# state @ w_in of batches 6 and 7: from a zero-padded stationary beside chunk 1 to eight float32 array tiles behind chunk 3

## The chip, the core and the metric

The kernel runs on one core of a Trainium2 chip. The metric is the device time of one execution in microseconds, the median of a few runs. Three runs of the kernel before took 663.02, 664.64 and 666.04 us. The core's engines work side by side, each through its own list of instructions in order: TensorE (PE, with its weight loads PEld), VectorE (DVE), ScalarE (ACT), GpSimd (POOL) and SyncE (SP), which issues nearly all DMAs.

## The reference

Attention between 512 tokens `x` and 32 state rows in both directions, for 8 batches and 8 heads, and then a feed-forward block over all rows.

```python
scores = x @ state^T / 8;  a  = softmax(scores);   xread = a  @ state   # B=8, H=8, S=512, D=64
scores2 = state @ x^T / 8; a2 = softmax(scores2);  sread = a2 @ x       # Ns=32
rows = concat([xread, sread])      # 544 rows a batch, 512 wide (8 heads x 64)
h = rows @ w_in                    # 512 -> 2048
out = (h - tanh(h)) @ w_out        # 2048 -> 512
```

## The kernel before

**What is multiplied.** For a token row, `xread @ w_in` is `a @ (state @ w_in)`. So the kernel makes `m = state @ w_in` for each batch (32 state rows by 8 heads, 2048 wide), and the first layer of a batch is `a @ m`: 256 rows are contracted where 512 would be. All products that need full precision are made from two float32r halves (`hi`, `lo`; `split`, line 99: a copy on ACT and a subtraction on DVE) as three matmuls.

**Chunks.** Batch i is chunk i. `Chunk.hidden(f)` (line 471) makes hidden block f of 16 with six matmuls of 128x512 (lines 483 to 485) into one of two `ps_h` banks, ACT takes tanh, DVE subtracts. `Chunk.output(f)` (lines 504 to 532) adds block f to four output banks with twelve matmuls. Chunks 0 to 3 run one after the other, step `st = 16 i + f`, two blocks ahead (`LAG`). Chunks 4 to 7 run in two `Pair`s (line 868) which share seven products instead of eight (`product`, line 944); their order is the list `ticks`. Chunk 8 holds the state rows of all batches.

**Where m comes from.** Blocks (q, k) of w_in, q = 0 to 3 and k = 0 or 1, are 128x1024 in the DRAM tiles `wf`. Batches 0 and 1 are done early: `m_first_two` (line 159) multiplies with plain float32 matmuls of 64 rows by 32 columns, four places in each of two banks of `ps_a`, eight instructions in all, followed by ACT copies. Batches 2 to 7 are done by `m_units` (line 205), 16 units, one for each (q, k, c): ACT and DVE split a 128x512 block of w_in (`wst`), six matmuls of 64x128 columns (line 232, `mps`) give batches 2 to 5, and three matmuls with the full array (line 239, `mls`) give batches 6 and 7. For these the stationary `sls` holds two heads on 128 rows with zeros where head and row do not belong together. ACT copies the banks out (`st`, line 197 through `free`; `sl`, line 241), and SP stores four pieces of `st` and four of `sl` to the DRAM tiles `md` (lines 247, 251). `load_m` (line 254) reads them back as `mr`, 512 KB for each (batch, q), and splits them to `m`. There is one `mr` buffer.

**What sets the order.** The program names a step for each side job: `ASIDE` (line 760) for chunks 0 to 3, `SIDES` (line 776) by tick for the pairs. A scheduler then orders the instructions of each engine by its own estimate, within priorities and explicit `issue_after` gates. `free` keeps all its ACT copies in one chain, and `behind_free` lets the first matmul of a group into `ps_a` wait for the last copy of that chain, since both banks must be free. The pools have few buffers: `stage` 2, `wf` 2, `x` 2 (tokens `xT` and `xn` of an attention, 512 KB each), `parts` 4 (the weights `W` of the pairs). SP issues DMAs in list order; one that waits holds all behind it. The attention of a batch is a generator: loads of `xT`, scores (`sps`, line 324, eight float32 matmuls of 64 rows by 32 columns), softmax, transposes (`pps`, line 410), loads of `xn`, the state read (`rps`, line 431).

Of the kernel before, what the change touches and what calls it, by code (L numbers as in the profile page):

```python
# [9 lines left out]
F32 = mybir.dt.float32  # L10
F32R = mybir.dt.float32r
# [8 lines left out]
P = 128  # L20
B, H, S, NS, D = 8, 8, 512, 32, 64
# [3 lines left out]
NQ = 4  # L25
# [6 lines left out]
TURN = (0, 1, 3, 2)  # L32
# [3 lines left out]
def attention_ffn(ctx: ExitStack, tc: tile.TileContext, xT, xn, bd, bh, sp, sm, sl, win, wout, xout, tout, sout):  # L36
# [62 lines left out]
    def split(hi, lo, src, sub=None):  # L99

        return nc.scalar.copy(hi, src), (sub or nc.vector).tensor_sub(lo, src, hi)  # L101
# [52 lines left out]
    def second(q):  # L154
        if q < 2:
            return pool.tile([P, 2, 512], F32, tag="stage", name=f"mr1{q}", bufs=SB)
        return pool.tile([P, 2, 512], F32, tag="g", name=f"mr1{q}", bufs=GB)

    def m_first_two(q, p):

        k = p // 2
        if p == 0:

            m_first[q] = pool.tile([P, 2, 512], F32, tag="mr", name=f"mr0{q}", bufs=RRB)
            m_second[q] = second(q)
        if p % 2 == 0:
            return
        pss = [bank(ps_a, f"mps0{q}{p - 1 + c}") for c in range(2)]
        run = []
        for b in range(2):  # L170
            for c in (1, 0):
                for e in range(2):
                    r = slice(64 * e, 64 * e + 64)
                    at = 64 * b + 32 * (e ^ c)
                    rows = slice(at, at + 32)
                    with ExitStack() as behind:
                        if run:
                            behind.enter_context(tc.issue_after(run[-1]))
                            behind.enter_context(tc.high_priority())
                        made = nc.tensor.matmul(  # L180
                            pss[c][rows], sps[r, p - 1 + c, rows], wfs[q, k][r, c], start=True, stop=True
                        )
                    if not run:
                        behind_free(made)
                    run.append(made.ins)
        for c in range(2):
            free(m_first[q][64 * c : 64 * c + 64, k], pss[c][0:64])
            free(m_second[q][64 * c : 64 * c + 64, k], pss[c][64:128])
# [16 lines left out]
    def m_units():  # L205
        raw = pool.tile([P, H, P], F32, tag="stage", name="smr", bufs=SB)
        s0 = pool.tile([P, 2, H, P], F32R, tag="sm", name="sms", bufs=1)
        nc.sync.dma_start(raw, sm)
        split(s0[:, 0], s0[:, 1], raw)
        raw = pool.tile([P, 4, P], F32, tag="stage", name="slr", bufs=SB)  # L210
        s1 = parts("sls", [P, 2, 4, P], F32R)
        nc.sync.dma_start(raw, sl)
        split(s1[:, 0], s1[:, 1], raw)
        for q in range(NQ):
            for k in range(2):
                w = pool.tile([P, 2, 512], F32, tag="wf", name=f"w1{q}{k}", bufs=WB)
                nc.sync.dma_start(w, wf[q][:, 2 * k : 2 * k + 2])
                for c in range(2):
                    p = 2 * k + c
                    t = twins(f"wst{q}{p}", [P, 2, 512], F32R)  # L220
                    split(t[:, 0], t[:, 1], w[:, c])
                    pss = [bank(ps_a, f"mps{q}{2 * p + e}") for e in range(2)]
                    ps2 = bank(ps_h, f"mls{q}{p}")
                    run = []
                    for n, (x, y) in enumerate(((0, 1), (0, 0), (1, 0))):
                        for e in (1, 0):
                            rows = slice(64 * e, 64 * e + 64)
                            with ExitStack() as behind:
                                if run:
                                    behind.enter_context(tc.issue_after(run[-1]))  # L230
                                    behind.enter_context(tc.high_priority())
                                made = nc.tensor.matmul(  # L232
                                    pss[e], s0[rows, x, 2 * p + e], t[rows, y], start=(n == 0), stop=(n == 2)
                                )
                            if not run:
                                behind_free(made)
                            run.append(made.ins)
                    for n, (x, y) in enumerate(((0, 0), (0, 1), (1, 0))):
                        nc.tensor.matmul(ps2, s1[:, x, p], t[:, y], start=(n == 0), stop=(n == 2))  # L239
                    late = pool.tile([P, 512], F32, tag="c2", name=f"sl{q}{p}", bufs=CSB)  # L240
                    nc.scalar.copy(late, ps2)
                    stage = pool.tile([P, 2, 512], F32, tag="stage", name=f"st{q}{p}", bufs=SB)
                    for e in range(2):
                        free(stage[:, e], pss[e])
                    for j in range(4):
                        dst = mdram[2 + j][q][k, 2 * c : 2 * c + 2]
                        nc.sync.dma_start(dst.rearrange("h n f -> n h f"), stage[32 * j : 32 * j + 32])
                    for e in range(2):
                        for j in range(2):
                            rows = slice(64 * e + 32 * j, 64 * e + 32 * j + 32)  # L250
                            nc.sync.dma_start(mdram[6 + j][q][k, 2 * c + e], late[rows])
                    yield

    def load_m(b, q):
        if b < 2:
# [33 lines left out]
    def attention(b, aT):  # L289
# [22 lines left out]
        def all_scores():  # L312

            pss.update({hf: bank(ps_a, f"sps{b}{hf}") for hf in range(2)})
            run = []
            for j in (2, 0, 3, 1):
                at = TURN[j] if b < 2 else j
                for hf in (1, 0):
                    rs = slice(64 * hf, 64 * hf + 64)
                    with ExitStack() as behind:  # L320
                        if run:
                            behind.enter_context(tc.issue_after(run[-1]))
                            behind.enter_context(tc.high_priority())
                        made = nc.tensor.matmul(
                            pss[hf][32 * at : 32 * at + 32], bdr[rs, j], xrs[j // 2][rs, j % 2], start=True, stop=True
                        )
                    if not run:
                        behind_free(made)
                    run.append(made.ins)
# [51 lines left out]
    def state_read(b, ss):  # L381
# [40 lines left out]
        for hf in range(2):  # L422
            for k in range(4):
                for c in range(4):
                    cs = slice(32 * c, 32 * c + 32)
                    j = TURN[c] if b < 2 else c
                    with ExitStack() as behind:
                        if run:
                            behind.enter_context(tc.issue_after(run[-1]))
                            behind.enter_context(tc.high_priority())  # L430
                        made = nc.tensor.matmul(  # L431
                            ps[cs, 64 * hf : 64 * hf + 64],
                            pts[hf][:, k, cs],
                            xrs[hf][:, k, 64 * j : 64 * j + 64],
                            start=(k == 0),
                            stop=(k == 3),
                        )
                    run.append(made.ins)
        for hf in range(2):
            for j in range(4):  # L440
                h = 4 * hf + (TURN[j] if b < 2 else j)
                js = slice(32 * j, 32 * j + 32)
                free(
                    sr[b // 4][32 * (b % 4) : 32 * (b % 4) + 32, 64 * h : 64 * h + 64],
                    ps[js, 64 * hf : 64 * hf + 64],
                    scale=ris[hf][js],
                )
# [308 lines left out]
    if "att0" in SCH:  # L756
# [3 lines left out]
    ASIDE = {  # L760
        "att1": D0["att"]["1"],
        "att2": [16 + x for x in (3, 4, 5, 6, 6, 8, 8, 9, 9)],
        "m0": [17, 18, 19, 20, 22, 23, 24, 25, 26, 27, 28, 29, 30, 31, 33, 34],
        "att3": [29, 30, 30, 31, 32, 33, 34, 35, 36],
        "a0": [37, 38, 38, 39],
        "att5": [39, 40, 40, 41, 42, 43, 44, 45, 46],
# [9 lines left out]
    SIDES = [  # L776
        {
            "att6": [0, 9, 14, 20, 26],
            "att7": [58, 61, 64, 67, 70, 73, 77, 81, 85],
        },  # L780
        {},
# [30 lines left out]
    def main(*made):  # L812
        mains[-1].extend(x.ins for x in made)

    late_units = {"a0": a0, "r1": late1, "m0": m1}

    def side(name, n=1):
        if not n:
# [290 lines left out]
```

## Time and profile before

| | |
|---|---|
| median of three runs | 664.64 us |
| profiled execution | 662.42 us, span 660.6 us, granted clock 0.992 |
| ACT busy | 389.2 us (59%), 675 instructions |
| PE busy | 633.5 us (96%), 3482 instructions |
| DVE busy | 483.8 us (73%) |
| DMA | 137.01 MB, mean 207 GB/s |
| lines 239 / 241 (`mls`) | 48 matmuls, 14.5 us; 16 ACT copies, 9.5 us |
| stores `md<-sl` / `md<-st` | 64 of 64 KB / 64 of 128 KB |

A row of the profile names line, engine, operation, tile written and tiles read. Times are microseconds from the span's start. A matmul of 128x512 is shown as 0.39 us long, but in a dense stream the next starts 0.23 us later, since matmuls are pipelined: PE time is read from start to start. A float32 matmul appears as two records in the trace. A row such as "x16" merges records that follow each other.

### The profile page before, as it was taken

The page shows a single profiled execution, that of the slowest core. Times are in us where ns is not written, and L with a number is a line of the kernel's source. Part 1 is how long each engine was busy: PE and PEld are TensorE (multiplying, and loading weights), DVE is VectorE, ACT ScalarE, POOL GpSimd, SP SyncE. Part 2 cuts the span into 40 slices and gives each one's busy share as a digit, 9 for nine tenths or more (in the row PEclk, how much of TensorE's full clock was granted, in tenths as well). Part 3 has the DMA queues.
Part 4 walks back from the last instruction along what each step waited for, and adds up shares of the span by engine and source line. Part 5 has one row for each costly group of instructions (what it writes and reads, how often), then busy time and mean ns, then how long its engine had stood idle before and what let it go on. Part 6 is the DMA issues. An engine that isn't in the chain of part 4 may idle for free.

```text
span 660.6 us, 9657 instructions
## 1 busy us (share of the span) xinstructions
PE 633.5 (96%) x3482; PEld 494.4 (75%) x3482; DVE 483.8 (73%) x769; ACT 389.2 (59%) x675; POOL 27.3 (4%) x41
## 2 busy tenths in 40 slices
PE   5879989999999999999999999999999999999997
PEld 2546667677777778787878887778888888788996
DVE  5999999639457876799637886996965789754442
ACT  3768875657667666576645576355655553543532
POOL 2000000000000000000000000000000000343300
PEclk9799999999999999999999999999999999999999
DMA  9799798356787974656722436464566535899800
GB/s 314 213 357 321 268 368 275 138 185 177 223 265 223 301 221 160 193 168 220 257 97 96 143 128 209 159 197 128 160 189 190 159 128 174 291 320 356 270 23 32
DMA packets 65199, 137.01 MB, mean 207 GB/s; under 512 B 6784, under 2 KB 28544, under 8 KB 65152
## 3 DMA queue, kind: packets, MB, share of 16 engines
q1 hardware_dynamic: 62592, 128.02, 59.5%
q0 software_dynamic: 2560, 8.39, 3.7%
q8 instruction: 27, 0.44, 0.3%
q14 instruction: 20, 0.16, 0.1%
HBM read 93.91 MB, written 42.47 MB: 206 GB/s over the span
## 4 chain that ended last, share of the span: by engine, by line
PE 77%; DVE 14%; DMA 4%; issue 3%; ACT 2%; SPq 0%; ACTq 0%; DVEq 0%
PE X L944 12%; PE hps L483 9%; PE hps L484 8%; PE hps L485 8%; PE ops L532 8%; PE ops L531 8%; PE ops L530 8%; PE Y1m L944 5%; PE Y0m L944 4%; PE mps L232 2%; PE mls L239 2%; PE rps L431 1%; DVE m L101 1%; DMA wo3d<-in_wout 1%; DVE w L131 1%
## 5 line engine op out<-in xcount | busy, mean ns | idle before, releaser
L531 PE MATMUL ops<-wo,g 128*128 128x512 f32 x256 | 99.9, 394 | 6.0 <-DVE wo L101 6.0
L483 PE MATMUL hps<-aT,m 128*128 128x512 f32 x248 | 99.3, 402 | 3.3 <-DVE G L497 1.3
L484 PE MATMUL hps<-aT,m 128*128 128x512 f32 x248 | 97.0, 391 | 0.0
L485 PE MATMUL hps<-aT,m 128*128 128x512 f32 x248 | 96.3, 391 | 0.0
L530 PE MATMUL ops<-wo,g 128*128 128x512 f32 x256 | 94.1, 396 | 0.9 <-ACT wo L101 0.8
L532 PE MATMUL ops<-wo,g 128*128 128x512 f32 x256 | 90.5, 394 | 0.0
L499 DVE TENSOR_TENSOR t<-hps,t 128x512 f32<-128x512 f32 (+1 forms) x78 | 49.5, 634 | 51.6 <-ACT t L499 51.3
L497 ACT ACTIVATE t<-hps 128x512 f32<-128x512 f32 x64 | 38.3, 599 | 61.8 <-PE hps L485 59.5
L497 DVE TENSOR_TENSOR G<-hps,t 128x512 f32<-128x512 f32 x64 | 43.9, 688 | 36.9 <-ACT t L497 36.9
L499 ACT ACTIVATE t<-hps 128x512 f32<-128x512 f32 (+1 forms) x78 | 43.3, 555 | 44.9 <-PE hps L485 42.3
L101 ACT CAST g<-t 128x512 fp32r<-128x512 f32 (+1 forms) x78 | 44.8, 579 | 32.0 <-DVE t L499 31.8
L483 PEld LDWEIGHTS hps<-aT,m 128*128 128x128 f32 x248 | 46.4, 188 | 22.9 <-ACT m L101 3.6
L531 PEld LDWEIGHTS ops<-wo,g 128*128 128x128 f32 x256 | 48.2, 188 | 19.0 <-DVE wo L101 8.3
L101 DVE TENSOR_TENSOR g<-t,g 128x512 fp32r<-128x512 f32 (+1 forms) x78 | 49.2, 633 | 14.8 <-ACT g L101 14.4
L530 PEld LDWEIGHTS ops<-wo,g 128*128 128x128 f32 x256 | 47.7, 188 | 16.4 <-ACT wo L101 3.0
L532 PEld LDWEIGHTS ops<-wo,g 128*128 128x128 f32 x256 | 48.2, 189 | 11.1 <-issue 0.8
L485 PEld LDWEIGHTS hps<-aT,m 128*128 128x128 f32 x248 | 46.5, 188 | 10.3 <-DVE m L101 0.4
L484 PEld LDWEIGHTS hps<-aT,m 128*128 128x128 f32 x248 | 46.6, 188 | 8.9
L982 POOL DMA_DIRECT2D wl<-wod x32 | 23.4, 730 | 590.9 <-DVE g1m L101 556.4
L944 PE MATMUL X<-g0m,W0m 128*128 128x512 f32 x192 | 46.9, 390 | 0.5 <-DVE g0m L101 0.5
L944 PE MATMUL X<-g1m,W1m 128*128 128x512 f32 x192 | 45.9, 391 | 0.6 <-DVE g1m L101 0.6
L101 ACT CAST g1m<-G 128x1024 fp32r<-128x1024 f32 x28 | 29.2, 1054 | 28.9 <-PE Y1m L944 12.7
(257 smaller groups left out, 1128.2 us busy)
## 6 DMA issues: line engine op xcount, KB each, us to landing
mr<-md SPq DMA_DIRECT2D x24, 512.0 KB, 3.8
xT<-in_xT SPq DMA_DIRECT2D x16, 512.0 KB, 4.9
wod<-wo SPq DMA_DIRECT2D x32, 256.0 KB, 6.1
md<-st SPq DMA_DIRECT2D x64, 128.0 KB, 2.4
xn<-in_xn SPq DMA_DIRECT2D x16, 512.0 KB, 5.3
wsd<-ws SPq DMA_DIRECT2D x16, 512.0 KB, 4.8
W0m<-wsd SPq DMA_DIRECT2D x16, 512.0 KB, 4.0
W1m<-wsd SPq DMA_DIRECT2D x16, 512.0 KB, 4.5
```

What stands on the lines that cost most here:

```text
L101: return nc.scalar.copy(hi, src), (sub or nc.vector).tensor_sub(lo, src, hi)
L232: made = nc.tensor.matmul(pss[e], s0[rows, x, 2 * p + e], t[rows, y], start=(n == 0), stop=(n == 2))
L483: nc.tensor.matmul(ps, mhi[k][:, cols], ahi[:, k], start=(k == 0), stop=False)
L484: nc.tensor.matmul(ps, mhi[k][:, cols], alo[:, k], start=False, stop=False)
L485: made = nc.tensor.matmul(ps, mlo[k][:, cols], ahi[:, k], start=False, stop=(k == nk - 1))
L497: main(nc.scalar.activation(t, ps, AF.Tanh), nc.vector.tensor_sub(g, ps, t))
L499: tanhs.append((nc.scalar.activation(t, ps, AF.Tanh).ins, nc.vector.tensor_sub(t, ps, t).ins))
L530: nc.tensor.matmul(o, g[:, 0, tok], w[:, 0], start=(f == 0), stop=False)
L531: nc.tensor.matmul(o, g[:, 0, tok], w[:, 1], start=False, stop=False)
L532: return nc.tensor.matmul(o, g[:, 1, tok], w[:, 0], start=False, stop=(f == NFF - 1)).ins
L944: made = nc.tensor.matmul(out[t], w[:, e, x, cols], y[:, e], start=first and j == 0 and e == 0 and c == 0, stop=last and j == 3 and e == 1 ...
L982: nc.gpsimd.dma_start(wo[f][:, :, cols].bitcast(F32), wod[:, f % 2, half, f // 2])
```

## The change

The three `mls` matmuls, the copy `sl`, its four stores and the padded stationary leave `m_units`. Batches 6 and 7 get a generator of their own, `m_last_two`, with a load step and then eight units, one for each (q, k). A unit has eight plain float32 matmuls of 64 rows by 32 columns into both `ps_a` banks (the code of `m_first_two`, now a function `eight`), two ACT copies of 128x512 into a `stage` tile, four stores of 128 KB, and the load of the next block of w_in (512 KB, `wf` pool). The stationary `spl` (128x256, not padded) lies in a buffer of the `x` pool. The units are asked for in the first pair's ticks 0 to 32, so the scheduler may place them from the end of chunk 3 on. The order of heads `TURN` that batches 0 and 1 had now holds for all batches, and the list of steps for the 16 units of `m_units` is 21 instead of 30 in one place.

```diff
-    def m_first_two(q, p):
+    def eight(name, held, w):
+        pss = [bank(ps_a, f"mps{name}{c}") for c in range(2)]
         run = []
         for b in range(2):
             for c in (1, 0):
...
-                        made = nc.tensor.matmul(
-                            pss[c][rows], sps[r, p - 1 + c, rows], wfs[q, k][r, c], start=True, stop=True
-                        )
+                        made = nc.tensor.matmul(pss[c][rows], held(c, r, rows), w[r, c], start=True, stop=True)
...
-        raw = pool.tile([P, 4, P], F32, tag="stage", name="slr", bufs=SB)
-        s1 = parts("sls", [P, 2, 4, P], F32R)
-        nc.sync.dma_start(raw, sl)
-        split(s1[:, 0], s1[:, 1], raw)
...
-                    ps2 = bank(ps_h, f"mls{q}{p}")
...
-                    for n, (x, y) in enumerate(((0, 0), (0, 1), (1, 0))):
-                        nc.tensor.matmul(ps2, s1[:, x, p], t[:, y], start=(n == 0), stop=(n == 2))
-                    late = pool.tile([P, 512], F32, tag="c2", name=f"sl{q}{p}", bufs=CSB)
-                    nc.scalar.copy(late, ps2)
...
-                    for e in range(2):
-                        for j in range(2):
-                            rows = slice(64 * e + 32 * j, 64 * e + 32 * j + 32)
-                            nc.sync.dma_start(mdram[6 + j][q][k, 2 * c + e], late[rows])
+    def m_last_two():
+        def held_w(q, k):
+            w = pool.tile([P, 2, 512], F32, tag="wf", name=f"w2{q}{k}", bufs=WB)
+            nc.sync.dma_start(w, wf[q][:, 2 * k : 2 * k + 2])
+            return w
+        spl = pool.tile([P, 4, 2, NS], F32, tag="x", name="spl", bufs=XB)
+        nc.sync.dma_start(spl, sl)
+        units = [(q, k) for q in range(NQ) for k in range(2)]
+        following = held_w(*units[0])
+        yield
+        for n, (q, k) in enumerate(units):
+            w = following
+            pss = eight(f"l{q}{k}", lambda c, r, rows: spl[r, 2 * k + c, rows.start // 64], w)
+            stage = pool.tile([P, 2, 512], F32, tag="stage", name=f"sl{q}{k}", bufs=SB)
+            for c in range(2):
+                free(stage[:, c ^ 1], pss[c ^ 1])
+            for b in range(2):
+                for c in range(2):
+                    dst = mdram[6 + b][q][k, 2 * c : 2 * c + 2]
+                    nc.sync.dma_start(dst.rearrange("h n f -> (h n) f"), stage[64 * b : 64 * b + 64, c])
+            if n < 7:
+                following = held_w(*units[n + 1])
+            yield
...
-        "m0": [17, 18, 19, 20, 22, 23, 24, 25, 26, 27, 28, 29, 30, 31, 33, 34],
+        "m0": [17, 18, 19, 20, 21, 22, 23, 24, 25, 26, 27, 28, 29, 31, 33, 34],
...
             "att6": [0, 9, 14, 20, 26],
+            "m6": [0, 4, 8, 12, 16, 19, 23, 29, 32],
...
-    late_units = {"a0": a0, "r1": late1, "m0": m1}
+    late_units = {"a0": a0, "r1": late1, "m0": m1, "m6": m_last_two()}
```

The change also moves instructions whose code it does not touch. In the rows below the numbers in a name are the program's own (`hps2_12` is hidden block 12 of chunk 2; `mps36`, `mps37` are the two banks of the last unit of `m_units`, q = 3), the number after the underscore is a running one, and the changed kernel's lines are 15 or 16 higher in this part of the file.

**First place, PE in chunk 2.** Before, the last matmul of the last unit of `m_units` is followed by hidden blocks 6 to 11 and outputs 4 to 9, some 106 rows, until the first matmul that reads `m23`, which that unit has to deliver:

```order
L232 MATMUL mps36_2297<-wst33_2294,sms_1134 128x512
L483 MATMUL hps2_6_2390<-aT2_1254,m21_2278 128x512
...
L532 MATMUL ops2_3_2197<-wo9_812,g2_9_2570 128x512
L483 MATMUL hps2_12_2736<-aT2_1254,m23_2733 128x512
L484 MATMUL hps2_12_2736<-aT2_1254,m23_2733 128x512
```

In the changed program the same unit stands behind output 9, and only outputs 10 and 11 (24 matmuls) and the transposes and state read of batch 3 are left between:

```order
L230 MATMUL mps36_2142<-wst33_2139,sms_1134 128x512
L545 MATMUL ops2_0_2049<-wo10_823,g2_10_2478 128x512
...
L547 MATMUL ops2_3_2052<-wo11_859,g2_11_2542 128x512
L425 MATMUL pps31_2198<-ident_72,s31_1918 128x128 x4
L425 MATMUL pps30_2197<-ident_72,s30_1916 128x128 x4
L446 MATMUL rps3_2238<-xn30_2193,p2t31_2209 32x64 x16
L446 MATMUL rps3_2238<-xn31_2195,p2t30_2207 32x64 x16
L498 MATMUL hps2_12_2571<-aT2_1229,m23_2568 128x512
```

The unit moved some five outputs later against hidden block 12, which itself now stands behind output 11 and not behind output 9.

**Second place, PE in the first pair.** The state read of batch 6 has two halves, `xn60` and `xn61`. Before, they stand together:

```order
L944 MATMUL X01_3816<-g0m130_3973,W0m13_3809 128x512
L431 MATMUL rps6_4112<-xn60_4025,p2t61_4041 32x64 x16
L431 MATMUL rps6_4112<-xn61_4027,p2t60_4039 32x64 x16
L483 MATMUL hps5_3_4043<-aT5_2614,m50_3959 128x512
```

In the changed program they stand 18 matmuls apart (six of `hps5_8`, six of a product, six of `hps5_9`), because `spl` holds one of the two `x` buffers and `xn61` goes into that of `xn60`:

```order
L446 MATMUL rps6_4065<-xn60_3959,p2t61_3975 32x64 x16
L498 MATMUL hps5_8_4130<-aT5_2449,m52_4062 128x512
...
L500 MATMUL hps5_9_4166<-aT5_2449,m52_4062 128x512
L446 MATMUL rps6_4065<-xn61_3961,p2t60_3973 32x64 x16
L498 MATMUL hps5_10_4177<-aT5_2449,m52_4062 128x512
```

**Third place, SP in the first pair.** Before, SP's list holds loads of `mr` and of pair weights `W0m` there:

```order
L259 DMA mr51_4010<-md51_94 128x2x512
L893 DMA W0m21_3924<-wod_77 128x1024
L893 DMA W0m22_3988<-wod_77 128x1024
L259 DMA mr52_4107<-md52_95 128x2x512
```

In the changed program the loads of w_in (`w2qk`) and the stores of the new units (`slqk`) stand among them; a store stands behind a weight load that waits until PE has used up a buffer:

```order
L264 DMA md60_97<-sl01_3745 64x512 x2
L264 DMA md70_101<-sl01_3745 64x512 x2
L274 DMA mr51_3925<-md51_94 128x2x512
L909 DMA W0m21_3820<-wod_77 128x1024
L247 DMA w220_3890<-wf2_107 128x1024
L264 DMA md61_98<-sl10_3811 64x512 x2
L264 DMA md71_102<-sl10_3811 64x512 x2
L247 DMA w221_3947<-wf2_107 128x1024
L909 DMA W0m22_3903<-wod_77 128x1024
L264 DMA md61_98<-sl11_3883 64x512 x2
```

Eight loads of 512 KB and 32 stores of 128 KB were added in this part, and 64 stores of 64 KB went from chunks 1 and 2.

More of the change, by code (lines that the diff above doesn't have):

```diff
@@ L157, in second @@
         return pool.tile([P, 2, 512], F32, tag="g", name=f"mr1{q}", bufs=GB)
-    def m_first_two(q, p):
[L161 to L168, printed above, removed]
+    def eight(name, held, w):
+        pss = [bank(ps_a, f"mps{name}{c}") for c in range(2)]
         run = []
@@ L185, in m_first_two @@
                     run.append(made.ins)
+        return pss
+    def m_first_two(q, p):
+        k = p // 2
+        if p == 0:
+            m_first[q] = pool.tile([P, 2, 512], F32, tag="mr", name=f"mr0{q}", bufs=RRB)
+            m_second[q] = second(q)
+        if p % 2 == 0:
+            return
+        pss = eight(f"0{q}{k}", lambda c, r, rows: sps[r, p - 1 + c, rows], wfs[q, k])
         for c in range(2):
@@ L237, in m_units @@
                             run.append(made.ins)
-                    for n, (x, y) in enumerate(((0, 0), (0, 1), (1, 0))):
-                        nc.tensor.matmul(ps2, s1[:, x, p], t[:, y], start=(n == 0), stop=(n == 2))
-                    late = pool.tile([P, 512], F32, tag="c2", name=f"sl{q}{p}", bufs=CSB)
-                    nc.scalar.copy(late, ps2)
                     stage = pool.tile([P, 2, 512], F32, tag="stage", name=f"st{q}{p}", bufs=SB)
                     for e in range(2):
-                        free(stage[:, e], pss[e])
+                        free(stage[:, e ^ c], pss[e])
                     for j in range(4):
@@ L316, in all_scores @@
             for j in (2, 0, 3, 1):
-                at = TURN[j] if b < 2 else j
+                at = TURN[j]
                 for hf in (1, 0):
@@ L425, in state_read @@
                     cs = slice(32 * c, 32 * c + 32)
-                    j = TURN[c] if b < 2 else c
+                    j = TURN[c]
                     with ExitStack() as behind:
@@ L440, in state_read @@
             for j in range(4):
-                h = 4 * hf + (TURN[j] if b < 2 else j)
+                h = 4 * hf + (TURN[j])
                 js = slice(32 * j, 32 * j + 32)
@@ L1085 @@
     sm = c(np.broadcast_to(sT[2:6].transpose(2, 1, 0, 3).reshape(1, D, H, P), (2, D, H, P)).reshape(P, H, P))
-    sl = np.zeros((2, D, 4, 2, 2, NS), x.dtype)
-    for e in range(2):
-        sl[e, :, :, e] = sT[6:, e::2].transpose(2, 1, 0, 3)
-    sl = sl.reshape(P, 4, P)
+    sl = c(sT[6:].reshape(2, 4, 2, D, NS).transpose(2, 3, 1, 0, 4).reshape(P, 4, 2, NS))
     win, wout = (c(w).view(np.int64) if w.dtype == np.float64 else w for w in (moe_w_in, moe_w_out))
```

## Prediction

> **What bounds the kernel now.** I read the page's busy times and slices first, then the busy time by stretches, then PE's timeline from start to start.
>
> ```profile
> PE 633.5 (96%) x3482; PEld 494.4 (75%) x3482; DVE 483.8 (73%) x769; ACT 389.2 (59%) x675; POOL 27.3 (4%) x41
> PE   5879989999999999999999999999999999999997
> PEclk9799999999999999999999999999999999999999
> PE 77%; DVE 14%; DMA 4%; issue 3%; ACT 2%; SPq 0%; ACTq 0%; DVEq 0%
> 120.00:240.00 120.00, 120.00 (x631) 88.70 (x629) 83.22 (x151) 81.73 (x152) 0.00 (x0) 1.00 0.71 217
> 340.00:400.00 60.00, 59.88 (x333) 48.01 (x336) 44.30 (x68) 37.96 (x65) 0.00 (x0) 1.00 0.38 132
> 400.00:446.00 46.00, 43.72 (x218) 33.99 (x206) 41.38 (x44) 23.51 (x36) 0.00 (x0) 1.00 0.61 196
> ```
>
> From the fifth line on each row is a stretch: its bounds and length, then the busy time of PE, PEld, DVE, ACT and POOL, the clock, the DMA share and GB/s. PE is busy throughout from 120 us on, at the full clock, and the chain that ended last is PE for 77% of the span. In 120 to 240 us, where the removed work lies, PE is busy 120.00 of 120.00 us: a matmul that goes there shortens the run. In 340 to 400 us, where most added work goes, PE has 0.12 us to spare: a matmul that comes there lengthens it. Only 400 to 446 us has room, 2.28 us, and there DVE is the busiest beside PE with 41.38 of 46 us. ACT and the DMAs are never full in these stretches. So the change is priced in PE's starts, and all else counts only where it makes PE wait.
>
> **What is removed.** The group and one of the 16 places, on PE's timeline (start, length, engine, line):
>
> ```profile
> L239 PE MATMUL mls<-wst,sls 128*128 128x512 f32 x48 | 14.5, 409 | 0.0
> 127.88 1.07 PE L532 MATMUL ops<-wo,g 128*128 128x512 f32 x4
> 128.79 0.84 PE L239 MATMUL mls<-wst,sls 128*128 128x512 f32 x3
> 129.47 0.39 PE L530 MATMUL ops<-wo,g 128*128 128x512 f32 x1
> L241 ACT COPY sl<-mls 128x512 f32<-128x512 f32 x16 | 9.5, 594 | 3.7 <-PE mls L239 3.5
> ```
>
> Three `mls` take 129.47 - 128.79 = 0.68 us, that is 0.227 us for each matmul of 512 columns, and the mean length of 409 ns in the group is no price, because lengths overlap. 16 x 0.68 = **10.9 us** leave PE. The 16 copies (9.5 us of ACT), the 64 small stores and the split of `sls` lie beside a full PE and count nothing.
>
> **What is added.** Eight units of eight float32 matmuls. The same shape stands in the trace as line 180 (`m_first_two`):
>
> ```profile
> 81.83 0.39 PE L485 MATMUL hps<-aT,m 128*128 128x512 f32 x1
> 82.15 1.09 PE L180 MATMUL mps<-w,sps 64*32 64x512 f32 x16
> 83.17 0.50 PE L530 MATMUL ops<-wo,g 128*128 128x512 f32 x1
> 83.50 0.39 PE L531 MATMUL ops<-wo,g 128*128 128x512 f32 x1
> L180 PE MATMUL mps<-w,sps 64*32 64x512 f32 x96 | 7.2, 659 | 1.1 <-ACT mr L197 1.1
> L197 ACT COPY st<-mps 128x512 f32<-128x512 f32 x32 | 17.2, 590 | 10.3 <-PE mps L232 5.6 <-issue 2.0 <-DMA md<-st 1.8
> ```
>
> The 16 records of the eight matmuls take 1.02 us together (82.15 to 83.17), so they run side by side. Around them lie 0.09 us (82.15 instead of 81.83 + 0.227) and 0.10 us (83.50 instead of 83.17 + 0.227). A unit is 1.02 + 0.09 + 0.10 = 1.21 us, and eight are **9.7 us**. The 16 added ACT copies (0.59 us each by the copies of `st`, 9.4 us) fall into 340 to 446 us, where ACT is busy 61.5 of 106 us; they are covered unless they hold a tanh, which is a rival below. The eight loads of w_in stand a unit ahead.
>
> The Trainium skill, "TensorEngine Tiling (Array Packing)", section "Key Properties", says that a change of tiling mode drains TensorE. That speaks against this change, since a removed `mls` mostly stood between full-array matmuls and changed no mode. The trace agrees, with the 0.19 us around the block; without the drain the added work would be 8.2 us.
>
> **What waits anew: m23.** In chunk 2 the last unit of `m_units` now stands just ahead of hidden block 12, which reads its result through DRAM. That round trip was run before, off PE's path:
>
> ```profile
> 235.56 0.96 PE L232 MATMUL mps<-wst,sms 64*128 64x512 f32 x6
> 236.94 1.07 ACT L197 COPY st<-mps 128x512 f32<-128x512 f32 x2
> 238.03 3.17 SPq L247 DMA_DIRECT2D md<-st  x4
> 241.31 0.38 SPq L259 DMA_DIRECT2D mr<-md  x1
> 245.40 1.05 ACT L101 CAST m<-mr 128x1024 fp32r<-128x1024 f32 x1 [2.73 <-DMA mr<-md]
> 172.90 1.03 PE L410 MATMUL pps<-ident,s 128*128 128x128 f32 x8
> 173.69 0.48 PE L483 MATMUL hps<-aT,m 128*128 128x512 f32 x1
> 178.63 1.10 PE L431 MATMUL rps<-xn,p2t 128*32 128x64 f32 x64
> 179.67 0.50 PE L483 MATMUL hps<-aT,m 128*128 128x512 f32 x1
> ```
>
> The block of six starts at 235.56; the longest of its kind passes PE in about 0.9 us, so it is through at 236.5, and the first half of `m` is there at 246.45: 10.0 us. Between unit and block 12 PE now has 24 matmuls (5.4 us), the transposes (173.69 - 172.90 = 0.8 us) and the state read (1.04 us, and 0.2 us around it): 7.4 us. PE is left waiting **2.6 us**. Bounds: 0 if stores and load take 2.6 us less (the copies here had four stores that took 3.17 us to issue), about 5 us if another `wsd` store or copy gets in between. I take the value in the row, since it is the very same transfer. Behind the waiting matmul stands everything on PE; ACT and DVE wait for its block, and output 12 behind it has a block and transposes as cover.
>
> **What waits anew: xn61.** It can be issued only when the first half of the state read has left its buffer, and the second half stands 18 matmuls later, 18 x 0.227 = 4.1 us.
>
> ```profile
> xn<-in_xn SPq DMA_DIRECT2D x16, 512.0 KB, 5.3
> 428.55 0.50 PE L483 MATMUL hps<-aT,m 128*128 128x512 f32 x1 [1.11 <-DVE G L497]
> 384.58 7.12 SPq L893 DMA_DIRECT2D W0m<-wod  x2
> md<-st SPq DMA_DIRECT2D x64, 128.0 KB, 2.4
> ```
>
> The last figure of the first and fourth row is the median time from issue to landing. 5.3 + 0.1 for the issue - 4.1 = **1.3 us** of waiting, with 0 below and some 3 above, if SP comes to it late.
>
> **What is given back.** In 400 to 446 us PE idles 2.28 us. The largest piece is the wait for DVE's G in the second row. DVE's work there does not change, but PE gets two units (2.4 us) and the wait for `xn61` more, and the scores of batch 7 leave. PE then comes later to what DVE has to deliver. I take **2.0 us** of the 2.28 as swallowed, between 0 and 2.28.
>
> **Sum.** -10.9 + 9.7 + 2.6 + 1.3 - 2.0 = +0.7 us. On the profiled execution (662.42 us, of which 660.6 is its span) that makes 663.1. It lay 2.2 us below the median of the runs, so against the median the sum is 664.64 + 0.7 = **665.3 us**.
>
> **Rivals.** *Nothing new waits.* The round trip of m23 is at least 2.6 us shorter, with 64 stores fewer on SP, and `xn61` lands in 4 us. Then -10.9 + 9.7 - 2.0 = -3.2, 661.4 us. For it: the DMA share is 0.71 in 120 to 240 us and falls. Against it: the load of `mr` alone took 4.1 us there (241.31 to 245.40), and the first store must land before it.
>
> *The copies hold the tanh; slower than before.* There are two `stage` tiles, so the copies of unit n + 2 wait until the four stores of unit n have landed. From unit 3 on these stand on SP behind a `W0m` load that waits for PE; in the trace a pair of such loads took 7.12 us where two issues are some 0.7 us, so 6.4 us were waiting. 6.4 + 4 x 0.43 for the stores + 2.4 to land = 10.5 us, and two units of distance are 2 x (18 x 0.227 + 1.2) = 10.6 us. From that point on each microsecond more keeps ACT from a tanh, and with two `ps_h` banks PE follows. With 1 us for each of units 4 to 8 on top it is +5, 670.3 us. Against it: most units stand farther apart. The Trainium skill, "TensorEngine Tiling (Array Packing)", section "Performance Considerations", warns that tiling speeds TensorE but not the emptying of PSUM, and that its copies may become the limit. That is this rival; the trace shows line 180 waiting for copies (`mr`, 1.1 us) at its early place, where the units follow faster.
>
> *It does not do what it says:* the eight do not run side by side when their weights are these. 16 records at 0.227 would be 3.6 us, 8 x 2.4 = +19, 684 us. Rows 82.15 and 83.17 speak against it.
>
> **How the numbers follow.** The forecast, with one or both waits and part of the return, gets 0.55, nothing waits 0.28, held tanh 0.15, no concurrency 0.02. A measurement here can tell about 0.5% from no change, 3.3 us. The forecast lies inside that band, with 0.05 below it and 0.04 above. The first rival lies on its edge: 0.15 below and 0.13 inside. The second gives 0.12 above and 0.03 inside, the third 0.02 above. So faster 0.20, same 0.62, slower 0.18. The range runs from 660.3 (nothing waits, and a microsecond beyond) to 669.8 (both waits at their upper bounds, +0.7 + 2.4 + 1.7 = 669.4), which leaves out the end of the second rival and the third.
>
> **What would show it.** The group `mls` is gone and PE's starts in chunks 1 and 2 are some 10 us denser. Each new unit takes 1.0 us from its first record to the next full matmul. In chunk 2 a hidden matmul waits for ACT's `m` behind a DMA of `mr`, 1 to 4 us; if PE does not stop there, that term is wrong. The second half of `rps` in the first pair starts some 5.5 us after the first with PE idle ahead of it. The waits for DVE's G around chunk 5's blocks 10 to 15 shrink below 1 us. I am wrong at the root if PE idles in many small pieces in the pair, with ACT's copies of `sl` ahead of tanh, or if the attention work that moved against chunk 2 and 3 makes DVE late there, which no row of before prices.

## The result, and the profile after

The changed kernel takes 667.1 us (median of 12 runs, 666.2 to 670.9), the kernel before 663.6 us (12 runs, 662.4 to 666.0). The ratio is 1.0056 with a 95% interval of 1.004 to 1.0071: 3.7 us slower, 2.7 to 4.7. The forecast was 665.3 us, +0.7; the range (660.3 to 669.8) holds the time. The change, 0.56%, lies just outside the 0.5% that was called no change, and its interval reaches inside.

The page of the changed kernel, engines and the chain that ended last, and below them its busy time by the stretches of before (bounds and length; PE, PEld, DVE, ACT, POOL; clock, DMA share, GB/s):

```profile
PE 632.9 (95%) x3562; PEld 485.9 (73%) x3562; DVE 483.7 (73%) x768; ACT 388.9 (58%) x674; POOL 26.9 (4%) x41
PE 73%; DVE 15%; DMA 6%; ACT 3%; issue 3%; SPq 1%; ACTq 0%; DVEq 0%
```

```profile
120.00:240.00 120.00, 119.04 (x624) 88.87 (x622) 80.78 (x137) 71.44 (x128) 0.00 (x0) 1.00 0.58 179
240.00:340.00 100.00, 95.53 (x754) 74.74 (x753) 79.84 (x163) 69.31 (x144) 0.00 (x0) 1.00 0.62 206
340.00:400.00 60.00, 59.12 (x324) 42.97 (x323) 40.50 (x64) 35.62 (x58) 0.00 (x0) 1.00 0.52 166
400.00:446.00 46.00, 46.00 (x308) 33.90 (x306) 39.43 (x42) 26.67 (x43) 0.00 (x0) 1.00 0.76 265
```

PE's busy total is nearly that of before, and the span is 4.5 us longer. The new idle time is in 240 to 340 us, 4.47 us in a stretch where before had none. In 400 to 446 us the 2.28 us of before are gone.

To see where the two runs part, the same three matmuls are looked up on PE's timeline: a hidden block of chunk 1 ahead of all removed work, hidden block 13 of chunk 3 ahead of all units, and a product behind them. First before, then after:

```profile
119.35 0.50 PE L483 MATMUL hps<-aT,m 128*128 128x512 f32 x1 [0.96 <-DVE t L499]
...
350.16 0.39 PE L484 MATMUL hps<-aT,m 128*128 128x512 f32 x1
...
565.92 1.43 PE L944 MATMUL X<-g1m,W1m 128*128 128x512 f32 x5 [0.58 <-DVE g1m L101]
```

```profile
121.54 0.50 PE L498 MATMUL hps<-aT,m 128*128 128x512 f32 x1 [0.96 <-DVE t L514]
...
346.92 0.39 PE L499 MATMUL hps<-aT,m 128*128 128x512 f32 x1
...
570.35 0.96 PE L960 MATMUL X<-g1m,W1m 128*128 128x512 f32 x3 [0.58 <-DVE g1m L101]
```

The changed kernel is 2.19 us late at the first, 3.24 us ahead at the second and 4.43 us late at the third. So the start costs 2.2 us, chunks 1 to 3 give **5.4 us**, and the pair costs **7.7 us**. The prediction had 8.3 and 9.0 for the two. The start is weighed at the end; the difference that matters lies in chunks 1 to 3. PE's waits there (240 to 345 us: engine, line, what it waited for; us in total, times, longest):

```profile
PE hps L498 <- ACT m L101: 1.8, 1, 1.8
PE hps L498 <- DVE G L512: 1.5, 1, 1.5
PE rps L446 <- ACT p2t L200: 0.7, 1, 0.7
PE hps L498 <- DVE t L514: 0.4, 1, 0.4
```

The first is m23, as predicted. The third is the state read that stands in m23's cover and waits for its own transposes. The second and the fourth were not in the sum. Together they are 4.4 us; 10.9 - 4.4 is 6.5, and 5.4 are seen. The other 1.1 us belong to the same four waits, since idle time is counted from the modelled end of a matmul and PE time goes from start to start. The wait for G:

```profile
327.26 0.39 PE L500 MATMUL hps<-aT,m 128*128 128x512 f32 x1
329.12 0.50 PE L498 MATMUL hps<-aT,m 128*128 128x512 f32 x1 [1.47 <-DVE G L512]
329.46 0.39 PE L499 MATMUL hps<-aT,m 128*128 128x512 f32 x1
```

329.12 - 327.26 is 1.86 us and the next step 0.34, where 0.23 each is usual: the wait costs 1.74 us. Read in the same way, m23 costs 2.25 us (inside hidden block 12 PE waits once more, 0.23 us, for the part of `m` that DVE makes), the state read 0.8 and t 0.6. That makes 5.4 us in all, so 10.9 - 5.4 = 5.5 should be left, and the places show 5.4.

### The profile page after: what moved, and what is told of

Read it like the earlier page. It is cut to its first block, busy times and chain, and to the rows that moved or that the text cites. A ratio compares the mean times of both kernels' runs of the same rounds, so it can differ in the third digit from the quotient of the medians.

```text
span 665.1 us, 9802 instructions
## 1 busy us (share of the span) xinstructions
PE 632.9 (95%) x3562; PEld 485.9 (73%) x3562; DVE 483.7 (73%) x768; ACT 388.9 (58%) x674; POOL 26.9 (4%) x41
## 4 chain that ended last, share of the span: by engine, by line
PE 73%; DVE 15%; DMA 6%; ACT 3%; issue 3%; SPq 1%; ACTq 0%; DVEq 0%
PE X L960 13%; PE hps L498 8%; PE hps L500 8%; PE hps L499 8%; PE ops L546 7%; PE ops L545 7%; PE ops L547 6%; PE Y0m L960 5%; PE Y1m L960 5%; PE mps L230 2%; DMA wf<-w 2%; DVE m L101 1%; DMA mr<-md 1%; DVE t L514 1%; DVE g L101 1%
## 5 line engine op out<-in xcount | busy, mean ns | idle before, releaser
L546 PE MATMUL ops<-wo,g 128*128 128x512 f32 x256 | 100.9, 398 | 7.7 <-DVE wo L101 7.7
L545 PE MATMUL ops<-wo,g 128*128 128x512 f32 x256 | 94.7, 398 | 0.9 <-ACT wo L101 0.8
L547 PE MATMUL ops<-wo,g 128*128 128x512 f32 x256 | 94.5, 397 | 0.0
L545 PEld LDWEIGHTS ops<-wo,g 128*128 128x128 f32 x256 | 47.7, 188 | 17.9 <-issue 3.5
```

The source lines that it names most:

```text
L545: nc.tensor.matmul(o, g[:, 0, tok], w[:, 0], start=(f == 0), stop=False)
L546: nc.tensor.matmul(o, g[:, 0, tok], w[:, 1], start=False, stop=False)
L547: return nc.tensor.matmul(o, g[:, 1, tok], w[:, 0], start=False, stop=(f == NFF - 1)).ins
```

## The experiments

All ratios are to the kernel before, with 95% intervals; a difference between two runs is taken from their ratios, unless medians are named. The theory from the trace (A) was: the removal is worth what PE's starts say, four waits born of the new order eat half of it (4.4 us of idle time, 5.4 from start to start), and the units cost their PE time less the waits of before that they cover. The rivals were the sum as predicted, and a late start that belongs to the build.

**The removal alone.**

```diff
-            "m6": [0, 4, 8, 12, 16, 19, 23, 29, 32],
...
-            nc.sync.dma_start(r, mdram[b][q].rearrange("g h n f -> (h n) g f"))
+            nc.sync.dma_start(r, mdram[b if b < 6 else b - 2][q].rearrange("g h n f -> (h n) g f"))
```

> The changed kernel without the eight units: state @ w_in of batches 6 and 7 is not made, and chunks 6 and 7 read the rows of batches 4 and 5 in its place. What is left of the change is the removal. Theory A (the trace of the changed kernel): between 120 and 345 us the removal takes about 9.9 us off the tensor engine and gives back 4.5 us in four new waits (1.87 for m23, 0.77 for a state read, 0.36 and 1.47 for the vector engine), so this kernel is 5.4 us faster than before, about -0.8%, and the eight units cost the rest, 7.6 to 9 us. Rival B (the sum as predicted): -10.9 + 2.6 = -8.3 us against before, -1.25%. Rival C: the changed kernel's 2.2 us of lateness at 55 us, where both kernels still have the same instructions, belongs to every build of it: then the fifth tanh starts near 57.5 us here too and the gain is only some 3.2 us, -0.5%; if it is chance, the fifth tanh may start anywhere between 55 and 58 us from run to run and the gain is 5.4 or more.

Measured: 659.96 us, ratio 0.9935 (0.9915 to 0.9954), 4.3 us faster (3.1 to 5.6). Rival B's 8.3 us are excluded. Between theory A (5.4) and rival C (3.2) the time does not decide: the fifth tanh did start late here, at 57.23 us, and the first place comes 3.56 us late, so the gain of chunks 1 to 3 has to be read from the places. The same three places on PE's timeline, and PE's waits from 345 to 450 us:

```profile
122.91 0.50 PE L498 MATMUL hps<-aT,m 128*128 128x512 f32 x1 [0.96 <-DVE t L514]
...
348.62 0.39 PE L499 MATMUL hps<-aT,m 128*128 128x512 f32 x1
...
564.36 1.42 PE L959 MATMUL X<-g1m,W1m 128*128 128x512 f32 x5 [0.58 <-DVE g1m L101]
```

```profile
PE hps L498 <- DVE G L512: 1.3, 2, 1.1
PE sps L339 <- ACT sr L200: 0.5, 1, 0.5
PE X L959 <- DVE g0m L101: 0.5, 1, 0.5
```

Chunks 1 to 3 give 5.1 us, and the pair takes what it took before (within 0.02 us). The four waits in 240 to 345 us are there again (1.9, 1.5, 0.7 and 0.7 us of idle time), so they come with the removal and not with the units. The pair's waits, 2.3 us, are those of before; in the changed kernel one of 0.9 us is left of them. So the units cover most of these waits, and their net cost is 7.7 us.

**Each unit's matmuls twice.**

```diff
-        for b in range(2):
+        for b in (0, 1) * (2 if name[0] == "l" else 1):
```

> The changed kernel, but each of the eight units makes its eight matmuls twice into the same banks, with nothing else added (same loads, copies and stores). If a unit is paid in full on the tensor engine, side by side at 1.02 us for eight, this is 8 x 1.02 = 8.2 us slower than the changed kernel, +1.2%. Rival: units lie partly in waits of the tensor engine (for the vector engine's G), then less than 6 us. Rival: they do not run side by side, then 16 us or more.

Measured: 678.0 us, 1.0192 (1.0165 to 1.0219), 9.0 us above the changed kernel (10.9 by the medians; the five runs lie between 674.5 and 678.6). A unit of the changed kernel and one of this run, each with the matmul behind it:

```profile
376.46 1.09 PE L173 MATMUL mpsl<-w,spl 64*32 64x512 f32 x16
377.48 0.50 PE L498 MATMUL hps<-aT,m 128*128 128x512 f32 x1
377.81 0.39 PE L499 MATMUL hps<-aT,m 128*128 128x512 f32 x1
```

```profile
379.28 1.95 PE L173 MATMUL mpsl<-w,spl 64*32 64x512 f32 x32
381.16 0.50 PE L498 MATMUL hps<-aT,m 128*128 128x512 f32 x1
```

A unit takes 1.02 us to the next full matmul (377.48 - 376.46), and that one 0.33 us to its successor, 0.10 more than usual. The second eight add 1.88 - 1.02 = 0.86 us, 6.9 us for eight units. Near 370 us PE waits 2.6 us for G, where the changed kernel waits 0.9: 1.7 us more. Together that is 8.6 us, and from the second to the third of the places this run takes 8.4 us longer than the changed kernel. So the second eight are paid in full on PE, side by side, and nothing of them hides.

**The raw states in another buffer.**

```diff
-        spl = pool.tile([P, 4, 2, NS], F32, tag="x", name="spl", bufs=XB)
+        spl = pool.tile([P, 4, 2, NS], F32, tag="ob", name="spl", bufs=OB)
```

> The changed kernel with the raw states of batches 6 and 7 in a buffer of the tag ob and not of the tag x, so that loads of xn61 and xT71 no longer wait for it; the state read of batch 6 is in one piece again and the scores of batch 7 are back before the long row of products. The prediction's term says 1.3 us faster than the changed kernel (0 to 3). Theory A (the trace of the changed kernel shows no wait of the tensor engine at that state read): no change, within 1 us; what the state read had as room it gets from the 18 matmuls between its halves.

Measured: 666.77 us, 1.0033 (1.0016 to 1.0049), 0.3 us below the changed kernel's median; by the two ratios 1.5 us, with intervals that overlap. The edit also moves the first unit behind chunk 3's last outputs, and the wait of 0.9 us near 370 us is gone. A wait for t near 285 us grew from 0.4 to 1.0 us instead, and from the first to the third of the places both kernels take 448.8 us. In the changed kernel the two halves of the state read stand so:

```profile
414.93 0.65 PE L446 MATMUL rps<-xn,p2t 128*32 128x64 f32 x32
...
419.82 0.65 PE L446 MATMUL rps<-xn,p2t 128*32 128x64 f32 x32
```

PE did not wait ahead of the second: the load was issued at 415.64 and was there 4.2 us later at most. The term of 1.3 us for `xn61` is 0.

**m23 from rows that are ready.**

```diff
-            nc.sync.dma_start(r, mdram[b][q].rearrange("g h n f -> (h n) g f"))
+            nc.sync.dma_start(r, mdram[b][2 if (b, q) == (2, 3) else q].rearrange("g h n f -> (h n) g f"))
```

> The changed kernel, but chunk 2's fourth quarter of hidden blocks is loaded from the rows of the third quarter, which were written long before; only that one load's source differs, so the product in chunk 2 is made with other numbers. The round trip of m23 then holds nobody. Theory A: the wait for it (1.87 us) goes, and with it some of the three other new waits (0.77, 0.36 and 1.47 us), since hidden blocks 12 and 13 no longer stand behind all outputs: 1.9 to 4.5 us faster than the changed kernel, -0.3 to -0.7%. Rival: another wait takes its place (the vector engine is busy 39 of the 40 us from 280 to 320 us), and the time stays that of the changed kernel within 1 us.

Measured: 673.81 us, 1.0141 (1.0118 to 1.0165), 5.6 us slower than the changed kernel. Both expectations missed. The wait for m23 is gone, but the scheduler, which now sees hidden block 12 ready early, puts all attention work of chunks 2 and 3 elsewhere, and PE waits for that (240 to 345 us):

```profile
PE pps L425 <- ACT sr L200: 2.7, 1, 2.7
PE hps L498 <- DVE t L514: 2.2, 1, 2.2
PE rps L446 <- DMA xn<-in_xn: 2.1, 1, 2.1
PE hps L498 <- DVE G L512: 1.4, 1, 1.4
PE pps L425 <- ACT s L200: 1.3, 1, 1.3
```

The granted clock was also 0.50 from 323.2 to 333.4 us, behind two of these waits, which adds to the loss. Such a run tells nothing of the price of m23. What it shows is how much the order of the side work is worth.

**Other steps for the sixteen units.**

```diff
-        "m0": [17, 18, 19, 20, 21, 22, 23, 24, 25, 26, 27, 28, 29, 31, 33, 34],
+        "m0": [17, 18, 19, 20, 21, 21, 22, 23, 23, 24, 25, 26, 27, 28, 29, 30],
```

> The changed kernel with other steps for the sixteen units (17, 18, 19, 20, 21, 21, 22, 23, 23, 24 to 30): the last one stands one output of chunk 2 earlier, the state read of batch 2 has moved from between it and hidden block 12 to behind block 14, and the two have 9.4 us of other work between them by the trace's durations (7.4 before). Theory A: the round trip of m23 takes 10.2 us as in the changed kernel, so the wait falls from 1.84 us to about 0.8 and the 0.73 us wait of that state read for its transposes goes: 1.8 us faster than the changed kernel, -0.25%. Rival: as in the run with m23 ready, the attention work that moves meets the vector engine full at 280 to 320 us and gives it back: no change or slower.

(The state read between the unit and block 12 is batch 3's, not batch 2's.) Measured: 675.25 us, 1.0162 (1.0137 to 1.0187), 7 us slower than the changed kernel: the rival, and far more of it. No wait for m23 is left, but the scores of a batch wait for their load, and transposes for ACT's softmax and for copies of the read ahead of them:

```profile
PE sps L339 <- DMA xT<-in_xT: 3.6, 1, 3.6
PE pps L425 <- ACT s L406: 1.8, 1, 1.8
PE pps L425 <- ACT sr L200: 1.5, 1, 1.5
```

**Batch 4's attention one step earlier**, an edit that moves only what stands around the wait for G near 329 us:

```diff
-        "att4": [46, 47, 47, 48, 49, 55, 56, 57, 59],
+        "att4": [45, 46, 46, 47, 48, 54, 55, 56, 58],
```

> The changed kernel with each step of batch 4's attention one step earlier. What moves is local: the state read that stood behind hidden blocks 10 and 1 now stands ahead of them, and the scores behind it come one output earlier. Theory A: the wait of 1.47 us for the vector engine's G at that place comes from order alone, three hidden blocks with no output between them on two banks; the state read (1.2 us) in that gap takes most of it, so the wait is 0.3 us or less and the kernel 1.2 us faster than the changed one, -0.2%. Rival: the vector engine is behind with attention work itself, G comes later by as much, and nothing changes.

Measured: 665.21 us, 1.0016 (1.0002 to 1.003), 2.7 us faster than the changed kernel (1.9 by the medians). The wait for G falls from 1.5 to 0.4 us with the same work on DVE, so it came from order alone. In this profile the gain was lost again: from the first to the third of the places above it takes 449.1 us, the changed kernel 448.8. From 260 us on, behind the wait for m23, PE ran at half speed, as the stretches of one microsecond show:

```profile
259.00:260.00 1.00, 1.00 (x4) 0.49 (x3) 1.00 (x1) 0.96 (x4) 0.00 (x0) 1.00 0.99 401
260.00:261.00 1.00, 0.93 (x3) 0.83 (x3) 0.34 (x3) 0.95 (x4) 0.00 (x0) 0.50 0.32 127
261.00:262.00 1.00, 1.00 (x4) 0.72 (x4) 0.32 (x2) 0.31 (x2) 0.00 (x0) 0.50 0.63 205
262.00:263.00 1.00, 1.00 (x4) 0.81 (x3) 0.18 (x1) 0.60 (x1) 0.00 (x0) 0.50 0.84 309
```

**All three of these edits together** (units earlier, batch 4 earlier, raw states apart), with no edit of its own:

> The changed kernel with the edits of the three runs together: units earlier, batch 4's attention one step earlier, the raw states of batches 6 and 7 in a buffer of their own. If the waits are separate, it is 2 to 3 us faster than the changed kernel, which puts it within 1 us of before, since the removal is worth 9.9 us and the eight units cost 7.5 to 9.4. If the waits only change places, it is as the changed kernel.

Measured: 675.52 us, 1.0163 (1.0136 to 1.0191). Neither expectation holds, and the waits are not separate: the edit of the sixteen units decides, and the other two give nothing on top of it.

**m23 stored first, on top of batch 4 earlier**, with the order on ACT and DVE kept:

```diff
+                        if q == NQ - 1 and p == 3 and j > 0:
+                            held_back.append((dst, stage[32 * j : 32 * j + 32]))
+                        else:
+                            nc.sync.dma_start(dst, stage[32 * j : 32 * j + 32])
...
+            while (b, q) == (2, 3) and held_back:
+                with tc.issue_after(made.ins):
+                    nc.sync.dma_start(*held_back.pop(0))
```

> The kernel with batch 4's attention a step early, and one thing more: the last of the sixteen units stores batch 2's rows first, and the stores of batches 3 to 5 are held back until the load of m23 has been issued. The order on the vector and the scalar engine is the same as without it, and on the tensor engine one matmul changes place. In the run without it the load was issued at 252.71 us, behind three stores of 0.59 us each. Theory A: the load starts some 1.8 us earlier, the first half of m comes 1.8 us earlier, and the wait of 2.05 us of hidden block 12 shrinks to about 0.3; the kernel is 1.8 us faster than the run without it, -0.27%, and so about 0.6 us faster than before, which the measurement cannot tell from it. Rival B: the transfer is bound by the DMAs' own time (the queue is shared, 0.7 busy there) and lands no earlier: no change. Rival C: the wait goes but another takes its place within chunk 2, as in the runs that moved attention work: no change or slower.

Measured: 664.75 us, 1.0011 (0.9996 to 1.0026), 0.3 us faster than the run without it (0.5 by the medians), which these intervals can't tell from nothing; 1.8 us was expected. The wait for m23 fell from 2.05 to 1.46 us, not to 0.3. SP's queue and ACT:

```profile
250.00 0.30 SPq L246 DMA_DIRECT2D md<-st  x1
251.09 0.52 SPq L832 DMA_DIRECT2D wsd<-ws  x1
252.87 0.38 SPq L279 DMA_DIRECT2D mr<-md  x1
...
257.48 1.04 ACT L101 CAST m<-mr 128x1024 fp32r<-128x1024 f32 x1 [1.51 <-DMA mr<-md]
```

SP was free at 251.61, and the load still left at 252.87, 2.87 us after the store's issue: it waits until the store has landed, at 252.79. Then it takes 4.6 us itself. In the run without the edit the load left at 252.71 us, right after the first store had landed at 252.47, though three more stores had been issued between. So those stores were hardly on the path; neither A nor B had that.

**The raw states apart as well**, on top of that.

> The same with the raw states of batches 6 and 7 in the tag ob too, which lets the first unit stand behind the last outputs of chunk 3: the wait of 0.7 to 0.9 us for G near 370 us goes, as in the run with that edit alone, where no wait was left between 340 and 450 us. Theory A: 0.7 us faster than the run with m23 stored first, that is 2.5 us faster than batch 4 a step early alone and 1.3 us faster than before (-0.2%). Rival: the gain lies within the noise because the vector engine's waits near 428 us, which the units of this place covered, come back.

Measured: 664.39 us, 1.0004 (0.9988 to 1.002), the time of before. No wait of PE is left from 345 to 450 us, as expected, but 0.36 us of gain is within the noise, and a wait for DVE's t near 285 us is 1.6 us here.

**m23 in two halves, and batch 5's attention two steps earlier**, on top of the last run.

```diff
+            halves = [slice(k, k + 1) for k in range(2)] if (b, q) == (2, 3) else [slice(0, 2)]
+            for ks in halves:
+                made = nc.sync.dma_start(r[:, ks], mdram[b][q].rearrange("g h n f -> (h n) g f")[:, ks])
...
+            for k in range(2):
+                split(m[:, 0, k], m[:, 1, k], r[:, k])
...
-        "att5": [39, 40, 40, 41, 42, 43, 44, 45, 46],
+        "att5": [37, 38, 38, 39, 40, 41, 42, 43, 44],
```

> The kernel with all local edits, and two things more: m23 is loaded and split in two halves, of which the first depends on units 13 and 14 only, so hidden blocks 12 and 13 begin with their first halves while the second half is still on its way; and batch 5's attention is two steps earlier, which keeps the distances between state reads that the kernel without this has. Theory A: the wait of 1.4 us for m23 goes, and the 0.7 us wait of a state read beside it, since outputs now stand between; 1.5 to 2 us faster than the kernel with all local edits, so about 1 us faster than before (-0.1 to -0.3%). Rival: the attention work that moves meets the vector engine at 280 to 320 us, its wait there (1.6 us) grows, and the time stays.

Measured: 662.14 us, 0.9974 (0.9957 to 0.999): **faster than before**, by 1.7 us (0.7 to 2.9), and 5.4 us faster than the changed kernel. From the first to the third of the places it takes 445.1 us, the kernel before 446.6. Hidden blocks 12 and 13 begin on the first half with outputs between. PE's waits in 240 to 345 us:

```profile
PE hps L512 <- ACT m L101: 1.2, 1, 1.2
PE hps L512 <- DVE G L526: 0.4, 1, 0.4
```

The wait for m23 is only 0.2 us shorter than with the load in one piece; what went are the 0.7 us of the state read in its cover and the 1.6 us for t. Both are gone in the next run too, so they went with the halves and the order that these bring.

**The same with batch 5's attention where it was.**

> The same without the two steps for batch 5's attention: three state reads now stand close together behind outputs 8 of chunk 3, as in the two runs that were 8 to 11 us slower. Theory A: the distance of the state reads is what made those runs slow (each needs loads through the two x buffers and copies that the next one waits for); this run shows new waits of a state read for loads or copies ahead of 340 us and is 2 us or more slower than its neighbour. Rival: the distance does not matter, what made them slow was the place of batch 3's state read in chunk 2; then it is as its neighbour within 1 us.

Measured: 669.01 us, 1.0071 (1.0046 to 1.0096), 6.4 us slower than its neighbour. PE's waits in 240 to 345 us, and SP's in 300 to 330 us:

```profile
PE rps L460 <- DMA xn<-in_xn: 3.5, 1, 3.5
PE hps L512 <- ACT m L101: 1.1, 1, 1.1
PE hps L512 <- DVE G L526: 0.4, 1, 0.4
```

```profile
SPq L331 <- PE rps L460: 8.9, 1, 8.9
SPq L923 <- DMA wsd<-ws: 4.6, 2, 4.0
```

What theory A forecast came: a state read waits 3.5 us for its load, and the run is more than 2 us slower. The place of batch 3's read is the same in both runs, so the rival is out. The mechanism holds in part. The first row shows the two `x` buffers: the load for the next scores waits 8.9 us until a state read has let go of them. But the load that the read at 325.28 us waits for left SP at 319.27, when the scores had let go of the buffers at 312.5; it stood behind a `W0m` load that waited 4.0 us for a store of `wsd` to land. Behind the wait of 3.5 us the granted clock was 0.50 for another 3.4 us.

**Before, profiled again.**

> The kernel before, profiled a second time. Both kernels have the same instructions on every engine up to about 100 us, yet the fifth tanh with a full bank started at 55.27 us in the profile of before and between 55.4 and 57.5 us in the twelve profiles of the changed kernel and its variants. Theory A: that is chance from run to run, and here it starts later than 55.3, somewhere in 55.3 to 57.5, with the rest of the run unchanged (PE idle near 409, 417, 428 and 440 us for 0.7, 0.3, 1.3 and 0.6 us). Rival: the start belongs to the build; then it is within 0.1 us of 55.27 again, and some 1 us of the changed kernel's slowness has no cause found in its trace.

Measured: 663.52 us, 1.0002 (0.9989 to 1.0015). The fifth tanh of a full bank on ACT, here and in the changed kernel:

```profile
54.38 0.60 ACT L499 ACTIVATE t<-hps 128x512 f32<-128x512 f32 x1 [0.19 <-PE hps L485]
```

```profile
57.45 0.60 ACT L514 ACTIVATE t<-hps 128x512 f32<-128x512 f32 x1 [0.49 <-PE hps L500]
```

54.38 us is outside what either side had written, so neither expectation holds as it stands; the waits of the pair are the same to 0.01 us.

## Why the prediction came out as it did

- **-10.9 us for 48 `mls`** holds as PE time: 5.4 us are seen, and the four waits cost another 5.4 from start to start. Half of the 16 places stood right behind a unit's six `mps` and not between full-array matmuls, as the prediction says of most; the 0.1 us behind the six then falls to the matmul that follows, and the price stays.
- **+9.7 us for eight units** holds: 1.02 us and 0.10 on either side, as in the rows quoted. Doubling them showed the price to be real. The rule on the change of mode (the Trainium skill, "TensorEngine Tiling (Array Packing)", "Key Properties") fits: those 0.10 us stand on both sides of a unit, and a second eight in the same mode costs 0.86 us.
- **+2.6 us for m23** holds. The trip took 10.2 us from the end of the unit to the first half of `m` (10.0 were written), and PE was idle for 1.8 us, plus 0.7 us for the state read that was counted as cover without a wait of its own; from start to start that is 3.0 us.
- **+1.3 us for xn61** is 0: the load was there in time. What the prediction left out is that the state read in two halves takes 0.3 us more.
- **-2.0 us given back** is about 2.4 us. PE's idle time in the two stretches fell from 2.40 to 0.88 us; from start to start the five waits of before cost 3.55 us there and the one that is left 1.15. Without units they stand as before. 9.7 + 0.3 - 2.4 is 7.6, and the pair cost 7.7.
- **Held tanh and no concurrency** did not come. ACT's `sl` copies waited 1.8 us for PE and never for a store.

The failing step is the list of what waits anew. It held m23 and xn61 alone, and put the attention work that the scheduler had moved in chunks 2 and 3 at nothing; the prediction's last sentence names that as the sign of being wrong. That work brought two waits for DVE, G and t, of 1.9 us idle and 2.4 us from start to start. With 3.0 for 2.6, no xn61, 0.3 for the two halves and 2.4 given back, the sum is -10.9 + 9.7 + 3.0 + 2.4 + 0.3 - 2.4 = +2.1, and the traces show +2.2 us from the first place on. That the range held owes something to luck: a wait of 1.3 us that did not come stood in for part of the 2.4 that were not priced. That it was order was shown by the runs: the waits are there without the units, batch 4 one step earlier took 1.1 us off one of them, and batch 5 two steps earlier made 6.4 us, though that last figure holds a stretch at half clock.

The ratio says 3.7 us and not 2.2. The rest lies in the start and in the clock, and is settled only in part. The fifth tanh started at 54.4 and 55.3 us in two profiles of before, and at 55.4 to 57.5 us in twelve profiles of the changed kernel and its variants, though the instructions up to there are the same, and on PE, ACT and DVE are the same up to the first place. The granted clock differs there: its mean in 40 to 60 us is 1.00 and 0.91 in the two profiles of before, and 0.83 in that of the changed kernel, where it was 0.50 from 47.7 to 54.5 us. It does not explain all of the starts, and whether the build plays a part stays open. And the twelve runs of the changed kernel had a granted clock of 0.989 on average, those of before 0.992 in the later comparisons; 0.003 of the span is 4 us more at 0.50. Within the runs of before, 0.989 goes with 665.0 us and 0.997 with 663.3, so that 0.003 is about 0.6 us. New waits may well bring such stretches, as they did in the profiles of several variants; the changed kernel's own profile shows none there.

## What to carry to other kernels

When PE is full, taking matmuls out is worth their starts only if what the scheduler puts in other places stays covered: compare the order of the side work as closely as the work itself, above all what stands between the maker of a value and its reader. The way of a value through DRAM was hardly shortened by clearing the queue behind its store, and letting the reader begin with the half that is there took only 0.2 us off its wait; the kernel before had independent matmuls between, and no wait. Experiments that take a dependency away change the order too; one that leaves the order as it is tells more.

## What the runs showed of the hardware

- A wait of PE can cost more than itself. Behind waits of some 1.4 to 3.6 us PE's granted clock was 0.50 for 3.4 us in some profiles (10.2 us in one place), with 0.43 us from matmul to matmul and not 0.23. The eight matmuls ahead of the transposes behind m23's wait took 1.97 us in the changed kernel's profile, where the clock stayed at 1.00 behind 1.84 us of waiting; they took 3.47 us with batch 4 earlier and 3.39 us with m23 stored first. In each of the two runs at 675 us it happened twice behind 280 us. The same wait is not always followed by it: one of 1.5 us near 112 us stands in all fourteen profiles, and the clock fell behind it in five. The Trainium skill, "TensorE: Matmul & The Clock Gate", "What's actually happening", says that the clock is halved after an idle window of about 3.4 us; here waits shorter than that were enough in some runs, and the measurement decides.
- A load that reads what a store has just written left SP only when the store had landed, 2.87 us after its issue, with the queue free for 1.26 us.
